# Moving VectorE work between slots in a fused spectral filter and two-layer GELU network, and one tile's second layer without the seven-product scheme

## The chip, the cores and the metric

The kernel runs on one core of a Trainium2 chip. The metric is device time in microseconds (us). The time before is 750.82 us, the median of three runs (750.49 to 752.01). A profiled execution of the same program took 750.39 us, and its span, from the first instruction to the last, is 748.6 us. Engines are named as in the profile: PE is TensorE's matmul, PEld its weight load, DVE is VectorE, ACT is ScalarE, POOL is GpSimd and SP is SyncE. "L468" is line 468 of the kernel before.

## The reference

```
x: 8 x 3008 x 256, filt_r and filt_i: 1505 x 256, w_in: 256 x 2048, w_out: 2048 x 256
X = rfft(x, axis=1);  Y = X * (filt_r + 1j*filt_i);  y = irfft(Y, n=3008, axis=1)
h = y.reshape(24064, 256) @ w_in
g = 0.5 * h * (1 + erf(h / sqrt(2)))
out = g @ w_out
```

## The kernel before

**Tiles and slots.** The Fourier transforms are matmuls with tables, in stages: 3008 = 47 x 64. The two layers run over 47 tiles of 512 tokens. A tile's first layer is 16 pieces (`mm1`, L637): two 128x512 matmuls into a PSUM bank of the pool "h" (three banks), and a gelu on ACT (L640) into `g_sb`. Each piece is a *slot*; slot 16*t + jc holds piece jc of tile t, and beside it a share of the second layer of tile t-1. In a slot first the steps that `put` listed for it are issued, then the second layer's share, then `mm1`. All engines take their instructions in the order of issue, and nothing reorders them.

**Second layer.** Tile 0 goes through `mm2_first` (L642): 64 matmuls of 256 columns, into two banks of the pool "o" (two banks), which L654 copies out. Every other tile goes through `mm2_seven`: the product is cut into two by two blocks and made with seven block products, 112 matmuls of 128 columns (L709), seven to a slot. For it VectorE forms sums of `g_sb` (`sums_1` L678 four times, `sums_2` L684 twice, `sums_3` L691 twice a tile) and adds the products up (L724, L726, L729, L731, L732, L735 and L738 twice a tile), which also frees the "o" banks. `put_rows` (L756) stores 128 rows at a time through the queue of SP or POOL.

**Spectral stages.** Batch 0 is transformed before slot 0. Batches 1 to 7 are spread over the slots, and are wanted by the tile that holds their rows; `first(b)` is the first slot of that tile. For a batch b:
- `load_next` (POOL) fetches x of the following batch; a tiny copy, `gate` (L146), makes POOL wait for a product of the unit before it starts a load.
- `fold` (L107 and L108, four per batch) forms sum and difference of two halves of x on VectorE.
- `s1` (L430, four per batch) is the first matmul stage; VectorE (L328) and ACT evict it, and SP stores it to DRAM. `r1` reads it back in another order (`b_sb`).
- `s2` (L457, three units per batch) is the second stage. It fills one "h" bank and all three banks of the pool "f". `s2_out` (four per unit) multiplies each bank with the filter (L468, into tiles `p`), and after the second of a pair forms the complex product sums (L471 and L472).
- `s3` (L485, one per unit) is the first inverse stage, again into one "h" bank and three "f" banks; `s3_out` evicts two banks at a time on ACT (L326; one bank of batch 1's unit 1 on VectorE) and stores them through SP. `r2` reads them back (`d_sb`).
- `s4` (L512, 16 per batch) is the last stage, into one "f" bank each; it is evicted by ACT or VectorE into `y_sb`, which `mm1` reads.

`s2[u]` below is the slot of unit u's s2. Before, s2 of batch 1 stands at slots 33, 45 and 57, and s3 at 42, 55 and 66. For batches 3 to 6 the units are 16 slots apart and s3 comes 10 slots after s2.

**Tables.** `table_4_all` builds the last stage's table on POOL (L411 and L413), in four parts of two pieces. A piece is two multiplications and an addition of 96x376, so a part is six POOL instructions. The four parts stand at slots 15, 80, 96 and 112. Their temporary tile comes from the pool that `d_sb` uses.

Of the kernel before, what the change touches and what calls it, by code (L numbers as in the profile page):

```python
# [22 lines left out]
TCH = 512  # L23
# [8 lines left out]
class _Mix:  # L32
# [428 lines left out]
    def s2_out(self, b, u, m, d):  # L461

        if d == 0:
            self.st[b, "p", 2 * u + m] = self.pp.tile([128, 2, 2, 2, 256], BF16, tag="p12", name="p12")
        w, a, v = self.st[b, "p", 2 * u + m], m ^ d, self.nc.vector.tensor_tensor
        ps = self.st[b, "ps2"][m][d].rearrange("p (r c) -> p r c", r=2)
        f = self.Fu[:, :, a, 2 * u + m, :]
        v(out=w[:, a], in0=ps.unsqueeze(2).to_broadcast([128, 2, 2, 256]),  # L468
          in1=f.unsqueeze(1).to_broadcast([128, 2, 2, 256]), op=ALU.mult)
        if d:  # L470
            v(out=w[:, :, 0, 0], in0=w[:, :, 0, 0], in1=w[:, :, 1, 1], op=ALU.subtract)  # L471
            v(out=w[:, :, 0, 1], in0=w[:, :, 0, 1], in1=w[:, :, 1, 0], op=ALU.add)  # L472

    def s3(self, b, u):

# [163 lines left out]
            o += n  # L639
        nc.scalar.activation(out=self.st["g", t][:, jc, :], in_=ps, func=AF.Gelu)  # L640

    def mm2_first(self, lo, hi):  # L642

        nc = self.nc
        for n in range(lo, hi):
            jc, q = (n // 2, n % 2) if n < 32 else (n % 16, n // 16)
            if n < 2:
                self.st["o2", q] = self.bank("ps_o", "o").rearrange("p (a b) -> p a b", a=2)
            ps = self.st["o2", q % 2]
            nc.tensor.matmul(ps[:, q // 2, :], lhsT=self.st["g", 0][:, jc, q * 128:q * 128 + 128],  # L650
                             rhs=self.w_out_sb[:, jc, :], start=(jc == 0), stop=(jc == 15))
# [41 lines left out]
    def mm2_seven(self, t, lo, hi):  # L693
# [9 lines left out]
        for n in range(lo, hi):  # L703
# [19 lines left out]
            if m == 0:  # L723
                nc.vector.tensor_copy(out=t1, in_=p1)  # L724
            elif m == 2:
                v(out=c(0, 0), in0=t1, in1=p0, op=ALU.add)  # L726
                if last:
                    self.store(t, 0, 0, nc.sync)
                v(out=t1, in0=t1, in1=p1, op=ALU.add)  # L729
            elif m == 4:  # L730
                v(out=t3, in0=t1, in1=p0, op=ALU.subtract)  # L731
                v(out=c(1, 1), in0=t3, in1=p1, op=ALU.add)  # L732
                if last:
                    self.store(t, 1, 1, nc.scalar)
                v(out=t1, in0=t1, in1=p1, op=ALU.add)  # L735
            else:
                for h, tt, p in ((1, t3, p0), (0, t1, p1)):
                    v(out=c(h, 1 - h), in0=tt, in1=p, op=ALU.add)  # L738
                    for sub in range(2):
                        self.put_rows(t * TCH + 256 * h + 128 * sub, self.st["c"][h][:, sub],  # L740
                                      nc.gpsimd if t > 1 or h > sub else nc.sync)
# [36 lines left out]
def kernel(  # L778
# [134 lines left out]
    for b in range(1, B):  # L913
        hi = first(b)
        e = 4 * (b == B - 1)
        s1, n1, r1 = (4, 2.75, 16) if b == 1 else (hi - 87, 3.7, hi - 73) if b == 2 else (hi - 94 - e, 3.7, hi - 80 - e)
        s2 = (33, 45, 57) if b == 1 else (hi - 64 - 2 * e + (b == 2), hi - 48 - 3 * e + e // 4, hi - 32 - 3 * e)
        busy.update(range(s1 - 1, s1 + int(3 * n1) + 2))
        for c in range(4):
            slot = s1 + int(c * n1 + (b == 1 and c in (1, 2)))  # L920
            put((0, 1, 5, 8)[c] if b == 1 else (67, 69, 86, 94)[c] if b == 2 else s1 - 28 + e + 6 * c, m.fold, b, c)
            put(slot, m.s1, b, c)
        for u in range(3):
            put(r1 if u < 2 else s2[0] + 1, m.r1, b, u)
            put(s2[u], m.s2, b, u)
            for i in range(4):
                put(s2[u] + ((0, 2, 5, 6)[i] if b == u == 1 else 2 * i + (b == 2 and u == 0)), m.s2_out, b, u, i // 2, i % 2)
            s3 = s2[u] + (9 if b == 1 and u != 1 else 10)
            put(s3, m.s3, b, u)
            put(s3 + 1, m.s3_out, b, u, 1)  # L930
            busy.update(range(s2[u] - 1, s2[u] + 5), range(s3 - 1, s3 + 2))
        after[b] = s3 + (5 if b > 1 else 4)
        crowd.update(range(s2[0], after[b]), range(s1 + 66, s1 + 94))
        if b + 1 < B:
            for i, (u, o, p) in enumerate(((0, 5, 1), (0, 7, 1), (1, 1, 2), (1, 5, 3), (1, 7, 3), (2, 1, 4), (2, 5, 5), (2, 7, 5))):
# [30 lines left out]
    put(14, m.table_4_factors, g)  # L966
    put(18, m.table_u)
    parts = [(w, h) for w in range(0, HB, 8) for h in range(2)]
    for i, slot in enumerate((15, 80, 96, 112)):
        put(slot, m.table_4_all, parts[2 * i:2 * i + 2])  # L970
    put(1, m.load_filters_again, nc.gpsimd, 0, 2)
    put(18, m.load_filters_again, nc.sync, 2, 4)
    put(20, m.weight_sums)
    seven = range(1, NT)
    for t in seven:
        for i, s in enumerate((12, 13, 15, 16 if t == S // TCH - 1 else 17)):
            put(16 * t + s, m.sums_1, t, 2 * i)
# [5 lines left out]
    for s in range((NT + 1) * 16):  # L983
# [43 lines left out]
```

## Time and profile before

| what | value |
|---|---|
| median of three runs | 750.82 us |
| profiled execution, its own time | 750.39 us |
| span of that execution | 748.6 us |
| PE busy | 730.8 us, 98% |
| PEld busy | 508.9 us, 68% |
| DVE busy | 616.9 us, 82% |
| ACT busy | 575.1 us, 77% |
| POOL busy | 288.2 us, 39% |
| granted TensorE clock | 1.00 |
| DMA | 89.31 MB, mean 119 GB/s |

A row of the costliest groups reads: line, engine, operation, what it writes and reads, the shape, how often, the busy time together, the mean duration of one, and the time the engine was idle just before such instructions with what ended most of it. A row of the timeline reads: start and length in us, engine, line, operation, tiles and shape, how many are merged into the row, and in brackets the idle time just before it and what ended it. Matmul durations overlap: the ends are modelled, and the next one starts long before the last one ends, so the rate is read from the starts.

### The profile page before, as it was taken

To read this page: it belongs to the slowest core of one execution; us is meant where nothing else is said; L and a number is where in the kernel's file an instruction comes from. 1 tells how busy PE (TensorE), PEld (TensorE's weight loads), DVE (VectorE), ACT (ScalarE), POOL (GpSimd) and SP (SyncE) were. 2 spreads that over 40 slices of the span, in tenths; PEclk is the share of its full clock that TensorE was granted. 3 is DMA by queue.
4 is the path that set the end of the run, shared out by engine and by line. 5 is a ranking of instruction groups with operands and counts; after the bars stand their busy time and mean duration, and the time that the engine had idled before them with its cause. 6 is when DMAs were issued, how large, how long until landed. Compare 5 with 4: busy or idle time off the path is not lost.

```text
span 748.6 us, 22400 instructions
## 1 busy us (share of the span) xinstructions
PE 730.8 (98%) x9261; PEld 508.9 (68%) x9261; DVE 616.9 (82%) x1120; ACT 575.1 (77%) x1048; POOL 288.2 (39%) x544
## 2 busy tenths in 40 slices
PE   8999999999999999999999999999999999999997
PEld 4856666666777667666677666666767766777776
DVE  8977998899887998789977989769997898676566
ACT  6987777677887788878887777877878787777773
POOL 7893446666122552234431355114631122112121
PEclk9999999999999999999999999999999999999999
DMA  9996542745345552546535455355444433301011
GB/s 154 213 193 185 125 109 86 212 90 123 86 121 177 117 119 82 142 148 134 112 103 162 111 126 131 90 158 129 117 108 118 153 91 99 117 31 58 29 57 58
DMA packets 81353, 89.31 MB, mean 119 GB/s; under 512 B 13171, under 2 KB 60659, under 8 KB 81251
## 3 DMA queue, kind: packets, MB, share of 16 engines
q0 software_dynamic: 22352, 39.76, 23.1%
q1 hardware_dynamic: 58483, 47.93, 22.8%
q8 instruction: 72, 1.18, 0.7%
q14 instruction: 30, 0.25, 0.1%
q10 hardware_dynamic: 416, 0.20, 0.1%
HBM read 55.57 MB, written 48.23 MB: 139 GB/s over the span
## 4 chain that ended last, share of the span: by engine, by line
PE 77%; DVE 15%; DMA 3%; POOL 2%; issue 2%; ACT 0%; DVEq 0%; POOLq 0%; SPq 0%
PE ps_h L637 35%; PE ps_o L709 33%; DVE p L468 5%; DMA x_sb<-in_x_dram 3%; PE ps_s L512 2%; PE ps_s L430 2%; DVE s_sb L678 2%; POOL out_dram L756 1%; PE ps_s L485 1%; DVE p L472 1%; PE ps_s L457 1%; DVE g_sb L684 1%; PE ps_o L650 1%; DVE s_sb L691 1%; DVE x_sb L108 1%
## 5 line engine op out<-in xcount | busy, mean ns | idle before, releaser
L640 ACT ACTIVATE g_sb<-ps_h 128x512 f16<-128x512 f32 x752 | 447.9, 603 | 146.1 <-PE ps_h L637 142.5
L637 PE MATMUL ps_h<-y_sb,w_in_sb 128*128 128x512 bf16 (+3 forms) x1600 | 445.3, 366 | 0.2 <-DVE a_sb L328 0.2
L756 POOL DMA_DIRECT2D out_dram<-ost x228 | 129.4, 574 | 389.3 <-DVE ost L738 359.4
L709 PEld LDWEIGHTS <-g_sb 128*128 128x128 f16 x2944 | 193.9, 98 | 90.1 <-issue 13.5
L709 PEld LDWEIGHTS <-s_sb 128*128 128x128 f16 x2208 | 147.8, 98 | 56.7 <-issue 3.7
L709 PE MATMUL ps_o<-w_sums,g_sb 128*128 128x128 f16 x1472 | 127.5, 219 | 4.7 <-DVE t_sb L729 3.5
L637 PEld LDWEIGHTS <-w_in_sb 128*128 128x128 bf16 x1600 | 125.0, 98 | 8.5 <-issue 1.1
L709 PE MATMUL ps_o<-w_sums,s_sb 128*128 128x128 f16 x1472 | 126.2, 219 | 0.1
L709 PE MATMUL ps_o<-w_out_sb,g_sb 128*128 128x128 f16 x1472 | 119.4, 219 | 2.1 <-DVE ost L738 2.1
L678 DVE TENSOR_TENSOR s_sb<-g_sb 128x1024 f16<-128x1024 f16 x184 | 120.3, 687 | 0.8 <-ACT g_sb L640 0.8
L468 DVE TENSOR_TENSOR p<-ps_s,F 128x1024 bf16<-128x1024 f32 x84 | 102.1, 1217 | 3.5 <-PE ps_s L457 1.8
L99 POOL DMA_DIRECT2D x_sb<-in_x_dram x156 | 79.0, 513 | 2.4 <-DMA x_sb<-in_x_dram 0.8
L684 DVE TENSOR_TENSOR g_sb<-s_sb,g_sb 128x1024 f16<-128x1024 f16 x92 | 65.0, 707 | 1.6
L709 PE MATMUL ps_o<-w_out_sb,s_sb 128*128 128x128 f16 x736 | 63.9, 219 | 0.0
L691 DVE TENSOR_TENSOR s_sb<-g_sb 128x1024 f16<-128x1024 f16 x92 | 63.8, 693 | 0.0
L731 DVE TENSOR_TENSOR t_sb<-t_sb,ps_o 128x256 f32<-128x256 f32 x46 | 19.3, 419 | 40.9 <-PE ps_o L709 39.7
L326 ACT ACTIVATE v_sb<-ps_s 128x512 bf16<-128x512 f32 x83 | 45.5, 608 | 6.3 <-PE ps_s L485 5.7
L326 ACT ACTIVATE y_sb<-ps_s 128x376 bf16<-128x376 f32 x94 | 46.6, 496 | 4.6 <-PE ps_s L512 4.6
L512 PEld LDWEIGHTS <-d_sb 96*128 96x128 bf16 x448 | 31.2, 97 | 27.2 <-issue 2.2
L738 DVE TENSOR_TENSOR ost<-t_sb,ps_o 128x256 f32<-128x256 f32 x90 | 33.7, 415 | 18.1 <-PE ps_o L709 18.1
L328 DVE CAST a_sb<-ps_s 128x512 bf16<-128x512 f32 x54 | 34.7, 684 | 12.7 <-PE ps_s L430 12.4
L726 DVE TENSOR_TENSOR ost<-t_sb,ps_o 128x256 f32<-128x256 f32 x46 | 19.1, 416 | 24.7 <-PE ps_o L709 24.1
(156 smaller groups left out, 556.7 us busy)
## 6 DMA issues: line engine op xcount, KB each, us to landing
out_dram<-ost POOLq DMA_DIRECT2D x126, 128.0 KB, 2.7
b_sb<-R SPq DMA_DIRECT2D x21, 512.0 KB, 5.2
R<-v_sb SPq DMA_DIRECT2D x84, 128.0 KB, 2.6
d_sb<-R SPq DMA_DIRECT2D x56, 192.0 KB, 3.3
R<-a_sb SPq DMA_DIRECT2D x108, 96.0 KB, 2.2
x_sb<-in_x_dram POOLq DMA_DIRECT2D x48, 94.0 KB, 2.7
x_sb<-in_x_dram POOLq DMA_DIRECT2D x48, 48.0 KB, 2.7
x_sb<-in_x_dram POOLq DMA_DIRECT2D x12, 188.0 KB, 5.1
```

What stands on the lines that cost most here:

```text
L99: self.nc.gpsimd.dma_start(out=xt[64 * v + to:64 * v + to + m, h, 4 * c:4 * c + 4 * n, :], in_=xv[h][at:at + m, w:w + 4 * n, :])
L326: self.nc.scalar.activation(out=out, in_=in_, func=AF.Copy, scale=1.0 if scale is None else scale)
L328: self.nc.vector.tensor_copy(out=out, in_=in_)
L468: v(out=w[:, a], in0=ps.unsqueeze(2).to_broadcast([128, 2, 2, 256]), in1=f.unsqueeze(1).to_broadcast([128, 2, 2, 256]), op=ALU.mult)
L512: nc.tensor.matmul(ps[:, 94 * i:94 * i + 94], lhsT=d[:, (grp % 2) * 4 + i, 128 * half:128 * half + 128], rhs=self.T4a[:, 4 * grp + i, 0:2 ...
L637: nc.tensor.matmul(ps[:, o:o + n], lhsT=w[:, dc], rhs=self.ring[:, dc, off:off + n], start=(dc == 0), stop=(dc == 1))
L640: nc.scalar.activation(out=self.st["g", t][:, jc, :], in_=ps, func=AF.Gelu)
L678: self.nc.vector.tensor_tensor(out=self.st["s", t][:, i:i + 2], in0=a, in1=b, op=ALU.subtract)
L684: self.nc.vector.tensor_tensor(out=a21[:, k], in0=self.st["s", t][:, k, 0], in1=a22[:, k], op=ALU.add)
L691: self.nc.vector.tensor_tensor(out=self.st["s4", t][:, k], in0=a12[:, k], in1=s2[:, k], op=ALU.subtract)
L709: nc.tensor.matmul(ps[:, (m + 1) % 2, sub, :], lhsT=a[:, i, 128 * sub:128 * sub + 128], rhs=b[:, i], start=i == 0, stop=i == 7)
L756: eng.dma_start(out=out, in_=tile_[lo - r0:lo - r0 + n])
```

## The change

Seven edits, in one diff:
- The product sums leave `s2_out` and become a step of their own, `s2_sum`. For batches 2 to 6 both pairs stand at s2 + 9 and s2 + 10, behind all four products; for batches 1 and 7 at s2 + 7 and s2 + 9.
- `s3` moves to s2 + 13 for batches 2 to 6 and to s2 + 11 for batches 1 and 7 (before: s2 + 10, or s2 + 9 for units 0 and 2 of batch 1). The last-stage steps around it move by a few slots, because the list of busy slots moves.
- Batch 1's units stand at slots 30, 43 and 56 in place of 33, 45 and 57, and lose an exception for unit 1's products.
- The folds move: for batch 2 the first two from slots 67 and 69 to 70 and 74; for later batches to 20, 13, 8 and 6 slots before `first(b)` - 94, where they were 28, 22, 16 and 10 before s1.
- The last three table parts move from slots 80, 96 and 112 to 22, 45 and 52.
- Tile 2's second layer goes through `mm2_first`, four matmuls of 256 columns a slot, and needs no sums; its rows are stored through POOL.
- Of tile 1's row blocks three go through POOL's queue and one through SP's (before: one and three).

```diff
@@ s2_out
-        if d:
-            v(out=w[:, :, 0, 0], in0=w[:, :, 0, 0], in1=w[:, :, 1, 1], op=ALU.subtract)
-            v(out=w[:, :, 0, 1], in0=w[:, :, 0, 1], in1=w[:, :, 1, 0], op=ALU.add)
+
+    def s2_sum(self, b, p):
+
+        w, v = self.st[b, "p", p], self.nc.vector.tensor_tensor
+        v(out=w[:, :, 0, 0], in0=w[:, :, 0, 0], in1=w[:, :, 1, 1], op=ALU.subtract)
+        v(out=w[:, :, 0, 1], in0=w[:, :, 0, 1], in1=w[:, :, 1, 0], op=ALU.add)
@@ mm2_first
-    def mm2_first(self, lo, hi):
+    def mm2_first(self, t, lo, hi):
...
-            jc, q = (n // 2, n % 2) if n < 32 else (n % 16, n // 16)
-            if n < 2:
-                self.st["o2", q] = self.bank("ps_o", "o").rearrange("p (a b) -> p a b", a=2)
-            ps = self.st["o2", q % 2]
-            nc.tensor.matmul(ps[:, q // 2, :], lhsT=self.st["g", 0][:, jc, q * 128:q * 128 + 128],
+            if t:
+                q, jc = n // 16, n % 16
+            else:
+                jc, q = (n // 2, n % 2) if n < 32 else (n % 16, n // 16)
+            if jc == 0 and (q % 2 == 0 if t else q < 2):
+                self.st["o2", q // 2 if t else q] = self.bank("ps_o", "o").rearrange("p (a b) -> p a b", a=2)
+            ps, a = (self.st["o2", q // 2], q % 2) if t else (self.st["o2", q % 2], q // 2)
+            nc.tensor.matmul(ps[:, a, :], lhsT=self.st["g", t][:, jc, q * 128:q * 128 + 128],
                              rhs=self.w_out_sb[:, jc, :], start=(jc == 0), stop=(jc == 15))
-            if q > 1 and jc == 15:
+            if jc == 15 and (q % 2 if t else q > 1):
                 ost = self.po.tile([128, 2, 256], FP32, tag="ost", name="ost")
                 nc.vector.tensor_copy(out=ost, in_=ps)
-                for a in range(2):
-                    self.put_rows((q - 2 + 2 * a) * 128, ost[:, a], nc.sync)
+                for i in range(2):
+                    self.put_rows(t * TCH + ((q - 1 + i) if t else (q - 2 + 2 * i)) * 128, ost[:, i],
+                                  nc.gpsimd if t else nc.sync)
@@ mm2_seven
-                                      nc.gpsimd if t > 1 or h > sub else nc.sync)
+                                      nc.gpsimd if t > 1 or h * sub == 0 else nc.sync)
@@ the slots of a batch
-        s2 = (33, 45, 57) if b == 1 else (hi - 64 - 2 * e + (b == 2), hi - 48 - 3 * e + e // 4, hi - 32 - 3 * e)
+        s2 = (30, 43, 56) if b == 1 else (hi - 64 - 2 * e + (b == 2), hi - 48 - 3 * e + e // 4, hi - 32 - 3 * e)
...
-            put((0, 1, 5, 8)[c] if b == 1 else (67, 69, 86, 94)[c] if b == 2 else s1 - 28 + e + 6 * c, m.fold, b, c)
+            put((0, 1, 5, 8)[c] if b == 1 else (70, 74, 86, 94)[c] if b == 2 else hi - 94 - (20, 13, 8, 6)[c], m.fold, b, c)
...
-                put(s2[u] + ((0, 2, 5, 6)[i] if b == u == 1 else 2 * i + (b == 2 and u == 0)), m.s2_out, b, u, i // 2, i % 2)
-            s3 = s2[u] + (9 if b == 1 and u != 1 else 10)
+                put(s2[u] + 2 * i + (b == 2 and u == 0), m.s2_out, b, u, i // 2, i % 2)
+            for i in range(2):
+                put(s2[u] + (9 + i if 1 < b < B - 1 else 7 + 2 * i), m.s2_sum, b, 2 * u + i)
+            s3 = s2[u] + (13 if 1 < b < B - 1 else 11)
...
-        after[b] = s3 + (5 if b > 1 else 4)
+        after[b] = s3 + 4
@@ tables and tiles
-    for i, slot in enumerate((15, 80, 96, 112)):
+    for i, slot in enumerate((15, 22, 45, 52)):
...
-    seven = range(1, NT)
+    plain = (0, 2)
+    seven = [t for t in range(NT) if t not in plain]
...
-            m.mm2_first(n(s), n(s + 1))
+            m.mm2_first(0, n(s), n(s + 1))
+        elif t - 1 in plain:
+            m.mm2_first(t - 1, 4 * jc, 4 * jc + 4)
```

In the kernel after the change, `after[b]` (the slot where `r2` starts reading back) is 71 for batch 1 and, for batches 2 to 6, 161, 257, 353, 449 and 545; it was 70, 159, 255, 351, 447 and 543.

## The prediction

> **What bounds the kernel now.** I read the page's first part, then the busy time by stretch, then TensorE's timeline wherever a stretch falls short, and last the timelines of the engine named there.
>
> ```profile
> PE 730.8 (98%) x9261; PEld 508.9 (68%) x9261; DVE 616.9 (82%) x1120; ACT 575.1 (77%) x1048; POOL 288.2 (39%) x544
> ...
> 60.00:100.00 40.00, 37.90 (x522) 24.15 (x520) 36.86 (x62) 27.67 (x50) 13.25 (x28) 1.00 0.54 127
> 145.00:190.00 45.00, 42.53 (x595) 28.99 (x588) 42.51 (x70) 33.54 (x63) 29.06 (x54) 1.00 0.56 129
> 190.00:237.00 47.00, 47.00 (x599) 34.20 (x597) 36.10 (x70) 37.81 (x69) 9.47 (x17) 1.00 0.41 121
> ```
>
> Columns of the stretches: length, then busy PE, PEld, DVE, ACT, POOL, granted clock, DMA share, GB/s. TensorE is the bound: from 190 to 237 us it never rests. It falls short where VectorE is nearly full (36.86 of 40, 42.51 of 45). So only stalls of TensorE can be won, and TensorE's order of work is fixed: a stall removed shortens the end by itself.
>
> ```profile
> 89.74 0.91 PE L457 MATMUL ps_s<-b_sb,T2p 64*32 64x256 bf16 x32
> 134.03 0.51 PE L709 MATMUL ps_o<-w_sums,g_sb 128*128 128x128 f16 x6 [0.71 <-DVE g_sb L684]
> 153.63 0.33 PE L512 MATMUL ps_s<-T4a,d_sb 96*128 96x94 bf16 x4 [1.69 <-DVE p L468]
> 260.62 0.93 PE L485 MATMUL ps_s<-p,U 32*64 32x256 bf16 x32
> 276.10 0.75 PE L485 MATMUL ps_s<-p,U 32*64 32x256 bf16 x32
> 278.65 0.38 PE L709 MATMUL ps_o<-w_sums,g_sb 128*128 128x128 f16 x4 [0.71 <-DVE t_sb L729]
> ```
>
> In TensorE's timeline a bracket is idle time. Seven 128-column matmuls start within 0.39 us (56 ns each), while one lasts 219 ns, so a bracket hides another 0.16 us of the previous matmul's tail: 0.71 costs 0.87. A group that runs long shows a wait inside it: s3 takes 0.75 unhindered and 0.93 when it waits for the product sums.
>
> ```profile
> 131.42 2.55 DVE L684 TENSOR_TENSOR g_sb<-s_sb,g_sb 128x1024 f16<-128x1024 f16 x1
> 366.32 0.42 DVE L472 TENSOR_TENSOR p<-p 128x512 bf16<-128x512 bf16 x1
> 366.65 0.68 DVE L107 TENSOR_TENSOR xs<-x_sb 111x1024 bf16<-111x1024 bf16 x1
> 367.37 0.69 DVE L108 TENSOR_TENSOR x_sb<-x_sb 111x1024 bf16<-111x1024 bf16 x1
> 367.98 0.41 DVE L726 TENSOR_TENSOR ost<-t_sb,ps_o 128x256 f32<-128x256 f32 x1
> 368.43 0.42 DVE L729 TENSOR_TENSOR t_sb<-t_sb,ps_o 128x256 f32<-128x256 f32 x1
> ...
> 131.79 1.61 POOL L411 TENSOR_TENSOR tmp_sb<-t_sb 96x376 f32<-96x376 f32 x2
> 75.84 1.11 ACT L326 ACTIVATE v_sb<-ps_s 128x512 bf16<-128x512 f32 x2
> ```
>
> These name the causes. A sum of 0.69 took 2.55 beside POOL's table part, and TensorE lost 0.87 at 133 us. In each steady batch, sums and a fold stand ahead of the L726/L729 additions that free a PSUM bank.
>
> Stalls in the TensorE timeline, in us: **A** (60 to 100 us, batch 1) 0.79+0.42, 0.75, 0.71, 0.28, 0.34, 0.90 = 4.2. **B** (100 to 145) 0.59, 0.33, 0.87 = 1.8. **C** (145 to 190, batch 2) 1.85, 0.28, 0.17, 0.18, 0.17, 0.18, 0.87 = 3.7. **D** (batches 3 to 6) per batch one 0.87, one or two s3 waits of 0.18, as many waits of 0.17 for L724: 1.2+1.6+1.6+1.6 = 5.9, the batch-3 one smaller. **E** (batch 7) 0.06+0.89 = 0.95. Together 16.6.
>
> **The change, part by part.** VectorE issue distances, from starts in its timeline: L468 product 1.14, L471+L472 0.70, L678/L684/L691 0.60, a fold's two 1.33, the 256-column L7xx ones 0.34, the 512-column copy 0.60. TensorE's slot (two 512-column and seven 128-column matmuls) 0.82.
>
> *Tile 2 direct.* Removes 112 matmuls x 0.056 = 6.24 and adds 64 of 256 columns, which start 0.109 apart in tile 0 (L650): 6.98. Cost **+0.75** on TensorE. On VectorE 8 sums and 10 evacuations leave, two copies come: 4.8+3.4-1.2 = 7.0 us less between slots 44 and 64, where its work (by these prices about 42 us over slots 28 to 72, as much as TensorE's 42) was the bound. [...]
>
> *Batch 1's units at 30, 43, 56; s3 at +11.* s2 at slot 30 falls at 62.2; its b_sb landed by 60.98, so it doesn't wait. VectorE then has from 62.65: four products 4.6, tile 0's copy 0.6, four sums 2.4, L724 0.34, the first product sums 0.70, L691 0.6, L726/L729 0.75, second sums 0.70 = 10.7, to 73.35. POOL's second table part, now at slot 22, runs at 60 to 66 beside them. Parts delayed VectorE by 0.83 (L678 pair 2.11 instead of 1.28), 0.9 and 2.0 in before; I take 0.85, bounds 0 and 2.0. So the sums end at 74.2, s3's half follows to 74.7, wanted at 71.5+0.95: stall 2.2 (1.4 to 3.4). Next, s2 stands two slots after s3. It needs s3's last banks, which ACT empties as two evictions, a gelu, two evictions, 0.48 each. In before unit 2 was two slots behind s3 and L457 took 0.91 instead of 0.63, with the last eviction on VectorE; with it on ACT as here 0.28+0.48 = 0.76 (bounds 0.28 and 0.96, one gelu more). Unit 2 keeps VectorE's help: 0.2. Its second sums come 6.7 after slot 60, s3 wants them at 6.4: 0.35, plus 0.85 for the part moved to slot 52, which POOL reaches at about 90 behind part 45, a gate, loads and tile 1's rows: 1.2 (0.35 to 2.3). A after: 2.2+0.76+0.2+1.2+0.75 = 5.1 against 4.2: **+0.9** (-1.2 to +3.4).
>
> *Table parts gone from slots 80, 96, 112.* The 0.33 and 0.87 of B go; 0.59 is gelu to L678 to L684 to TensorE and stays: **-1.2** (-0.5 to -1.3).
>
> *Product sums behind all four products, s3 at +13 (batches 2 to 6).* The four sums (1.4) now stand behind L468, L726, L729, L691; from s2 on VectorE has 4.6 of products, three sums before the tile and two L691 3.0, L724 0.34, L726/L729 0.75, and then these 1.4 = 10.1, and TensorE takes 11.7 to s3 (s2 0.65, 13 slots 10.7, two s4 0.34), so L724's 0.17, s3's 0.18 and L729's 0.87 go. L729 would be late again only if four sums and a fold still stood ahead. What is late next is the next s2, three slots behind s3 (it was six). Such a spacing exists in before: s3 ended at 74.31, s2 started at 76.88, the last ACT eviction ended at 76.95, and s2 took its usual 0.63. I take 0.05 each for eight, D: 5.9-0.4 = **-5.5** (-5.9; or -1.6 if each costs one ACT eviction more, 0.48). Batch 2's first pair has only two slots: 0.76, and s4 at slots 118 to 124 follows the products that free its banks: 0.2 (0 to 0.9). C **-2.7** (-3.5 to -1.8).
>
> *Batch 7, sums at +7 and +9, s3 at +11.* One sum pair less ahead of L738 (0.89 to 0.2); a two-slot pair costs 0.76: E **0.0** (-0.8 to +0.5).
>
> *Folds* stay 14 slots or more ahead of s1, where VectorE's work over eight slots (five sums, a fold, L738 twice, L724) is 6.0 of TensorE's 6.6: 0. If that cover went, 1.33 would land on L738. *Queues:* tile 1's three row stores leave SP for POOL and wait behind part 45 (6.2 us); their four-deep ost buffers are wanted again at about 99, after landing by 91. POOL's gates and x loads behind them move some 8 us; the chunks wanted by the fold at slot 74 were loaded with gate 48, by 93: 0. SP loses a wait for L738. r2 is two slots later, and d_sb landed at 375.5 for s4 at 382.2, so 3 us remain: 0.
>
> [...]
>
> Sum: 0.9-1.2-2.7-5.5+0.0 = -8.5. From the profiled execution's 750.39 (span 748.6 and 1.8 around it) this is **741.9**; the median of the runs, 750.82, is 0.4 above that execution.
>
> **Rivals.** (1) *The steady gain half fails:* the L729 wait stays (4 x 0.87) and A ends at its worse bound (+2.5 more): 741.9+6.0 = 747.9. For it: four sums and two folds are only moved. Against: the order puts the sums after L726/L729. (2) *No gain:* the three-slot spacing costs 0.9 at each of nine places, 750. (3) *Slower:* s3's banks bind. The mechanism is one: ACT empties them too late for s2. If s4's evictions two slots earlier leave ACT two instructions and a gelu behind (1.44 at nine places, 13.0, less the 0.4 counted), the time is 754.5. It decides from 1.0 us per place (8.5/9 and the 0.05). Against: ACT rests 0.23 before nearly every gelu, and 76.88 shows no wait. (4) *More gain:* POOL meets no two-input sum, A at -1.2 and C, D, E at their lower ends: -12.7, 737.7.
>
> **How the numbers follow.** Forecast with its own range 738 to 745.5: 0.68. Rival 1 0.12, rival 2 0.05, rival 3 0.10, rival 4 0.05. Runs here differ by 0.2% (1.5 us), about what can be told from no change. Faster takes the forecast, rivals 1 and 4 less some of rival 1: 0.82; same 0.06; slower 0.12. Range 738 to 748: it leaves rivals 2 and 3 and a tail below.
>
> **What would show it.** s3 groups of 0.75 in batches 3 to 6 with no bracket on L729; no L684 of 2.5 at 130; L457 near 1.4 in the two-slot places and 0.63 to 0.7 in the three-slot ones; a bracket of 1 to 2 us at batch 1's first s3. Wrong if L457 runs long everywhere, if s4's L512 waits for d_sb, or if A loses more than 3.

## The result and the profile after

The changed kernel takes 741.12 us (median of four runs, 740.40 to 741.93). The kernel before has 751.41 us over four runs (the three given above and one of 752.26). The ratio is 0.9864 with a 95% interval of 0.9846 to 0.9881, so the change saves 10.3 us or 1.4% (9.7 us against the 750.82 of the first three). The profiled execution of the changed kernel took 740.78 us, its span is 739.0 us.

The line numbers move a little in the changed kernel: mm1 is L640, its gelu L643, the seven-product matmul L716, `s3` L488, `s4` L515, the product sums L474 and L475, `sums_1` to `sums_3` L685, L691 and L698, the additions of the seven-product scheme L731 to L745 (L736 was L729, L745 was L738), and `r2` L506. `s2` stays L457 and the product with the filter stays L468.

First the busy times of the changed kernel, from the page's first part:

```profile
PE 716.6 (97%) x9063; PEld 506.7 (69%) x9213; DVE 604.0 (82%) x1105; ACT 575.6 (78%) x1049; POOL 290.8 (39%) x547
```

Then its busy time by stretch, for the stretches that the prediction read and two more (columns as there: length, PE, PEld, DVE, ACT, POOL, granted clock, DMA share, GB/s):

```profile
60.00:100.00 40.00, 37.10 (x447) 24.03 (x462) 33.62 (x47) 27.00 (x48) 31.86 (x48) 1.00 0.47 116
100.00:145.00 45.00, 42.92 (x532) 29.23 (x535) 35.30 (x68) 34.26 (x64) 13.84 (x28) 1.00 0.52 141
145.00:190.00 45.00, 44.11 (x615) 30.97 (x625) 41.55 (x73) 36.27 (x68) 22.93 (x47) 1.00 0.56 120
190.00:237.00 47.00, 46.63 (x591) 34.21 (x596) 37.01 (x69) 37.03 (x69) 11.81 (x21) 1.00 0.47 137
```

From 145 to 190 us TensorE now works 44.11 of 45 us where it had 42.53, while VectorE is as full as it was (41.55 against 42.51): VectorE's work there is hardly less, it stands in another order. From 60 to 145 us VectorE has clearly less to do (33.62 and 35.30, before 36.86 and 38.01), POOL in the first of these stretches 18.6 us more, and TensorE does not gain. (TensorE's sums are a little low in these rows, since 150 matmul records, 146 of them of L640, are missing from this trace.)

Starts of the gelus give a sharper view, because slot N is the same piece of work in both kernels. The table is worked out from the gelu rows of the two timelines:

| part of the span | before | after | difference | forecast |
|---|---|---|---|---|
| start to slot 0 | 38.34 | 38.57 | +0.24 | 0 |
| slots 0 to 16 | 14.55 | 14.12 | -0.43 | 0 |
| A, slots 16 to 67 | 49.62 | 49.00 | -0.62 | +0.9 |
| B, slots 67 to 112 | 42.11 | 42.50 | +0.39 | -1.2 |
| C, slots 112 to 168 | 55.25 | 52.29 | -2.96 | -2.7 |
| D, slots 168 to 576 | 385.03 | 378.93 | -6.10 | -5.5 |
| E, slots 576 to 640 | 59.78 | 60.40 | +0.62 | 0.0 |
| slots 640 to 751 | 93.69 | 93.69 | 0.00 | 0 |
| last gelu to the end | 10.22 | 9.49 | -0.73 | 0 |
| span | 748.59 | 739.00 | -9.59 | -8.5 |

The last row but one is no gain of the mechanism: the last matmuls and stores are issued at the same distance from the last gelu in both kernels, and only the time from the last store's issue to the end of the span differs. That tail is 9.97 to 10.63 us in the three profiles built on the kernel before, 9.47 to 9.49 in ten of the eleven built on the changed kernel and 10.06 in the other; whether this is chance stays open. The first two rows scatter (38.3 to 39.9 and 14.1 to 15.2 us over the 14 profiles of this study). Without the three, 8.67 us are gained where 8.5 were forecast.

One border of the table is unfair. Gelu 67 starts 1.31 us after the first weight load of its own `mm1` in the kernel before and 0.75 us in the changed one, because ACT is later there. Taken at the weight load, so on TensorE's side, A is 0.06 us shorter and B 0.17 us shorter; their sum is the same.

What is left of TensorE's waits in the changed kernel, from its timeline (start, length, tiles, number of matmuls merged, and in brackets the idle time and its end):

```profile
69.17 0.51 PE L716 MATMUL ps_o<-w_sums,g_sb 128*128 128x128 f16 x6 [0.99 <-DVE g_sb L691]
74.15 0.65 PE L488 MATMUL ps_s<-p,U 32*64 32x256 bf16 x16 [0.88 <-DVE p L474]
77.42 0.41 PE L457 MATMUL ps_s<-b_sb,T2p 64*32 64x256 bf16 x15 [0.22 <-ACT v_sb L326]
89.61 0.82 PE L457 MATMUL ps_s<-b_sb,T2p 64*32 64x256 bf16 x32
114.68 0.33 PE L515 MATMUL ps_s<-T4a,d_sb 96*128 96x94 bf16 x4 [1.65 <-DMA d_sb<-R]
158.57 0.72 PE L457 MATMUL ps_s<-b_sb,T2p 64*32 64x256 bf16 x17
159.51 0.41 PE L457 MATMUL ps_s<-b_sb,T2p 64*32 64x256 bf16 x15 [0.22 <-ACT v_sb L326]
259.45 0.64 PE L488 MATMUL ps_s<-p,U 32*64 32x256 bf16 x32
262.59 0.63 PE L457 MATMUL ps_s<-b_sb,T2p 64*32 64x256 bf16 x32
551.73 0.33 PE L515 MATMUL ps_s<-T4a,d_sb 96*128 96x94 bf16 x4 [0.51 <-DMA d_sb<-R]
591.32 0.45 PE L716 MATMUL ps_o<-w_out_sb,g_sb 128*128 128x128 f16 x5 [0.66 <-DVE ost L745]
```

In the steady batches the waits of before are gone: `s3` takes 0.64 us at 259.45, and `s2`, three slots behind it, 0.63 us at 262.59. One small wait per batch is new: the `s4` at 267.48 starts 0.2 us late, just after the product L468 that ends at 267.43. The two-slot pairs at 77 and 159 wait for ACT; the one at 159 takes 1.35 us from 158.57 to 159.92 (two rows), 0.72 more than the 0.63 of an unhindered group. Two waits are of a kind that the profile of before did not have: `s4` waits for the DMA that brings `d_sb`, at 114.68 and 551.73.

VectorE's timeline of the changed kernel in batch 3 shows the order that does it:

```profile
256.14 0.42 DVE L736 TENSOR_TENSOR t_sb<-t_sb,ps_o 128x256 f32<-128x256 f32 x1
256.47 0.69 DVE L698 TENSOR_TENSOR s_sb<-g_sb 128x1024 f16<-128x1024 f16 x1
257.08 0.42 DVE L474 TENSOR_TENSOR p<-p 128x512 bf16<-128x512 bf16 x1
...
258.08 0.42 DVE L475 TENSOR_TENSOR p<-p 128x512 bf16<-128x512 bf16 x1
```

L736, the second of the two additions that free the PSUM bank, comes first; the four product sums (two rows left out) follow and end at 258.5, 0.95 us before `s3` wants them at 259.45.

### The profile page after: what moved, and what is told of

Read it like the earlier page. It is cut to its first block, busy times and chain, and to the rows that moved or that the text cites. A ratio compares the mean times of both kernels' runs of the same rounds, so it can differ in the third digit from the quotient of the medians.

```text
span 739.0 us, 22144 instructions
## 1 busy us (share of the span) xinstructions
PE 716.6 (97%) x9063; PEld 506.7 (69%) x9213; DVE 604.0 (82%) x1105; ACT 575.6 (78%) x1049; POOL 290.8 (39%) x547
## 4 chain that ended last, share of the span: by engine, by line
PE 87%; ACT 4%; DVE 3%; DMA 3%; issue 2%; POOL 0%; SPq 0%; another core or an unknown queue 0%; DVEq 0%; POOLq 0%; ACTq 0%
PE ps_o L716 38%; PE ps_h L640 37%; PE ps_s L515 3%; PE ps_s L430 2%; PE ps_o L656 2%; ACT g_sb L643 2%; PE ps_s L457 2%; PE ps_s L488 2%; DMA R<-v_sb 1%; ACT v_sb L326 1%; DVE p L468 1%; DMA d_sb<-R 1%; DMA x_sb<-in_x_dram 1%; PE ps_c L587 1%; ACT y_sb L326 1%
## 5 line engine op out<-in xcount | busy, mean ns | idle before, releaser
L643 ACT ACTIVATE g_sb<-ps_h 128x512 f16<-128x512 f32 x752 | 445.8, 603 | 141.1 <-PE ps_h L640 116.5
L640 PE MATMUL ps_h<-y_sb,w_in_sb 128*128 128x512 bf16 (+3 forms) x1454 | 414.4, 365 | 0.6
L763 POOL DMA_DIRECT2D out_dram<-ost x231 | 131.2, 575 | 398.5 <-DVE ost L745 390.0
L716 PEld LDWEIGHTS <-g_sb 128*128 128x128 f16 x2880 | 189.0, 98 | 84.5 <-issue 13.5
L716 PEld LDWEIGHTS <-s_sb 128*128 128x128 f16 x2160 | 145.0, 98 | 53.6 <-issue 3.7
L640 PEld LDWEIGHTS <-w_in_sb 128*128 128x128 bf16 x1600 | 125.7, 98 | 7.7 <-issue 1.3
L716 PE MATMUL ps_o<-w_sums,g_sb 128*128 128x128 f16 x1440 | 124.8, 220 | 2.4 <-DVE g_sb L691 1.0
L716 PE MATMUL ps_o<-w_sums,s_sb 128*128 128x128 f16 x1440 | 123.4, 219 | 1.7 <-DVE t_sb L731 0.2
L685 DVE TENSOR_TENSOR s_sb<-g_sb 128x1024 f16<-128x1024 f16 x180 | 119.5, 696 | 0.7 <-ACT g_sb L643 0.6
L716 PE MATMUL ps_o<-w_out_sb,g_sb 128*128 128x128 f16 x1440 | 116.5, 220 | 2.5 <-DVE ost L745 0.7
L468 DVE TENSOR_TENSOR p<-ps_s,F 128x1024 bf16<-128x1024 f32 x84 | 102.0, 1218 | 7.8 <-PE ps_s L457 6.2
L716 PE MATMUL ps_o<-w_out_sb,s_sb 128*128 128x128 f16 x720 | 62.5, 219 | 0.9
L691 DVE TENSOR_TENSOR g_sb<-s_sb,g_sb 128x1024 f16<-128x1024 f16 x90 | 62.1, 691 | 1.5
L698 DVE TENSOR_TENSOR s_sb<-g_sb 128x1024 f16<-128x1024 f16 x90 | 61.5, 683 | 0.0
L738 DVE TENSOR_TENSOR t_sb<-t_sb,ps_o 128x256 f32<-128x256 f32 x45 | 18.8, 419 | 41.6 <-PE ps_o L716 41.1
L515 PEld LDWEIGHTS <-d_sb 96*128 96x128 bf16 x448 | 31.2, 97 | 28.6 <-DMA d_sb<-R 2.8
L745 DVE TENSOR_TENSOR ost<-t_sb,ps_o 128x256 f32<-128x256 f32 x88 | 32.9, 416 | 15.6 <-PE ps_o L716 15.6
```

The costliest lines, as they stand in the source:

```text
L515: nc.tensor.matmul(ps[:, 94 * i:94 * i + 94], lhsT=d[:, (grp % 2) * 4 + i, 128 * half:128 * half + 128], rhs=self.T4a[:, 4 * grp + i, 0:2 ...
L640: nc.tensor.matmul(ps[:, o:o + n], lhsT=w[:, dc], rhs=self.ring[:, dc, off:off + n], start=(dc == 0), stop=(dc == 1))
L685: self.nc.vector.tensor_tensor(out=self.st["s", t][:, i:i + 2], in0=a, in1=b, op=ALU.subtract)
L691: self.nc.vector.tensor_tensor(out=a21[:, k], in0=self.st["s", t][:, k, 0], in1=a22[:, k], op=ALU.add)
L698: self.nc.vector.tensor_tensor(out=self.st["s4", t][:, k], in0=a12[:, k], in1=s2[:, k], op=ALU.subtract)
L716: nc.tensor.matmul(ps[:, (m + 1) % 2, sub, :], lhsT=a[:, i, 128 * sub:128 * sub + 128], rhs=b[:, i], start=i == 0, stop=i == 7)
```

## The experiments

All kernels but the first two start from the changed kernel. A median is given with that of the kernel before from the same session. The latter moved between 750.88 and 751.41 us from session to session, so a difference of medians from two sessions is good to about 0.5 us. Parts of the span are those of the table above.

**The product sums alone** (`sums_only`): the kernel before, with nothing changed but the sums of batches 2 to 6.

```diff
+            mid = 1 < b < B - 1
+            for i in range(2 if mid else 0):
+                put(s2[u] + 9 + i, m.s2_sum, b, 2 * u + i)
+            s3 = s2[u] + (13 if mid else 9 if b == 1 and u != 1 else 10)
...
-        after[b] = s3 + (5 if b > 1 else 4)
+        after[b] = s3 + (5 if b == B - 1 else 4)
```

> The kernel before, with the product sums of batches 2 to 6 behind all four products and s3 at s2 + 13; folds, tables, batch 1, batch 7 and tile 2 as before. Theory (the sums ahead of L726/L729 and right before s3 make the waits): the D waits go as in the forecast (-5.5 us), and of batch 2 the three s3 waits, two L724 waits and the L729 wait (1.75 together) less one two-slot s2 (0.6): about -6.6, 744.5 to 745. Rival (the fold ahead of L726/L729 makes the largest wait, and it stays where it was here): the five waits of 0.87 for L729 stay, so about -2.3, 749.

Measured: 743.24 us (before 751.05; ratio 0.9893, 0.9878 to 0.9908), 7.8 us of the 10.3, and 1.3 below the theory's range; the rival is out. Part D is 379.66 us, 5.37 less than before, and C 52.92, 2.33 less; A and B stay within 0.25 us of before. In its TensorE timeline the waits for L729 are gone, with the folds still at their old slots:

```profile
171.04 0.64 PE L490 MATMUL ps_s<-p,U 32*64 32x256 bf16 x32
...
191.24 0.45 PE L714 MATMUL ps_o<-w_out_sb,g_sb 128*128 128x128 f16 x5 [0.28 <-DVE ost L743]
```

A bracket of 0.28 (0.44 us with the hidden tail) remains at the end of a tile, at 191 and twice later, where a fold delays L743 (L738 in before). So the step of the sums carries most of the change, and the folds are not needed to free L729. The sums and the three slots by which `s3` moves come together here; no run has `s3` later alone.

**The table parts alone** (`tables_only`): the kernel before, with one line changed.

```diff
-    for i, slot in enumerate((15, 80, 96, 112)):
+    for i, slot in enumerate((15, 22, 45, 52)):
```

> The kernel before with one line changed: the three late table parts at slots 22, 45 and 52, where the prediction put -1.2 us on stretch B. Theory (the parts collide wherever VectorE is full): the waits of L729 at 113 and 121 and part of the one at 99 go (-1.2 to -1.8 us), but the parts of slots 22 and 45 stretch VectorE's work between 62 and 90 us, where the seven-product group of tile 2 still stands in this kernel, and TensorE waits 1 to 3 us more there. Sum -0.5 to +2: 750.5 to 753. Rival (the tables cost nothing in their new slots, as the prediction had it but for one 1.2 us wait): no new wait before slot 64, 749.3 to 749.9.

Measured: 752.99 us (before 750.88; ratio 1.0029, 1.0019 to 1.0039), slower by 2.1 us, at the upper end of the theory's range and far from the rival. A takes 55.35 us, 5.7 more than before, where the theory had 1 to 3; B 0.35 less and C 1.7 less. TensorE, VectorE and POOL in this kernel's timelines:

```profile
76.06 1.11 PE L485 MATMUL ps_s<-p,U 32*64 32x256 bf16 x26 [1.44 <-DVE p L468]
87.29 0.45 PE L709 MATMUL ps_o<-w_out_sb,g_sb 128*128 128x128 f16 x5 [2.00 <-DVE ost L738]
104.08 1.11 PE L485 MATMUL ps_s<-p,U 32*64 32x256 bf16 x26 [0.82 <-DVE p L468]
106.14 0.71 PE L709 MATMUL ps_o<-w_out_sb,g_sb 128*128 128x128 f16 x5 [0.74 <-DVE ost L738]
```

```profile
76.72 2.75 DVE L691 TENSOR_TENSOR s_sb<-g_sb 128x1024 f16<-128x1024 f16 x1
```

```profile
77.29 1.61 POOL L411 TENSOR_TENSOR tmp_sb<-t_sb 96x376 f32<-96x376 f32 x2
78.98 1.33 POOL L413 TENSOR_TENSOR T4a<-tmp_sb 96x376 bf16<-96x376 f32 x1
```

The sum, elsewhere 0.68 us, starts at 76.72 and lasts until 79.47, past both L411 and into L413. VectorE falls behind over this stretch, and L738 holds TensorE for 2.00 us at 87. The new slots are no place with little VectorE work in this kernel; in the changed kernel, with tile 2's second layer off VectorE, they still cost A 1.2 us (`tables_back` below).

**Tile 2 back to seven products** (`tile2_seven`):

```diff
-    plain = (0, 2)
+    plain = (0,)
```

> The kernel after, with tile 2's second layer through the seven products again. Theory (VectorE is the bound of batch 1's stretch): TensorE saves 0.75, but VectorE has 7.0 us more between slots 44 and 64 and TensorE waits for it again, 2 to 4 us, so +1.3 to +3.3, 742.4 to 744.4. Rival (VectorE has room there since the sums and tables moved): only the 0.75 is left, 740.4.

Measured: 743.21 us (before 751.05; ratio 0.9894, 0.9879 to 0.9908), 2.1 us more than the changed kernel and inside the theory's range. A is 3.6 us longer; B is 1.2 shorter, as this profile lacks the wait for `d_sb`. VectorE is late at three places of A, of which the changed kernel has the first (0.99 us there):

```profile
70.47 0.51 PE L716 MATMUL ps_o<-w_sums,g_sb 128*128 128x128 f16 x6 [1.28 <-DVE g_sb L691]
86.29 0.45 PE L716 MATMUL ps_o<-w_out_sb,g_sb 128*128 128x128 f16 x5 [1.17 <-DVE ost L745]
103.37 0.45 PE L716 MATMUL ps_o<-w_out_sb,g_sb 128*128 128x128 f16 x5 [1.00 <-DVE ost L745]
```

The direct layer costs TensorE 0.75 us by its rates and is worth 2.1 net.

**The folds back** (`folds_back`):

```diff
-            put(... (70, 74, 86, 94)[c] if b == 2 else hi - 94 - (20, 13, 8, 6)[c], m.fold, b, c)
+            put(... (67, 69, 86, 94)[c] if b == 2 else s1 - 28 + e + 6 * c, m.fold, b, c)
```

> The kernel after, with the folds at their old slots. Theory (sums): without the sums ahead of it a fold alone doesn't make L729 late, so at most +0.5, 741 to 741.6. Rival (folds): the L729 wait of 0.87 comes back in five batches, +4.4, 745.5.

Measured: 742.67 us (before 751.05; ratio 0.9886, 0.9871 to 0.9901), 1.5 us more, above the theory and far from the rival. L736 is not late. What comes back is one wait at the end of a tile in batches 2, 5 and 6, as in `sums_only`:

```profile
190.71 0.45 PE L716 MATMUL ps_o<-w_out_sb,g_sb 128*128 128x128 f16 x5 [0.27 <-DVE ost L745]
```

Three of 0.44 are 1.3 us. C and D are 0.62 and 1.19 us longer than in the changed kernel. The old and the new slots of the folds both leave L729 alone; the new ones also clear the tile's end.

**The table parts back** (`tables_back`):

```diff
-    for i, slot in enumerate((15, 22, 45, 52)):
+    for i, slot in enumerate((15, 80, 96, 112)):
```

> The kernel after with the table parts back at slots 15, 80, 96 and 112, all else as in after. Prediction's step: the moved parts were worth 1.2 us, so 742.3. Theory now (a part costs where it is put, as long as VectorE has little slack there): the 1.15 us wait at 68 and the 1.82 us wait for the second-spectrum transfer at 113 go, the 0.59 us wait under the latter shows again, and one or two waits of 0.3 to 0.9 us come back between 113 and 135 us. Sum -2.4 +0.6 to 1.5: 739.3 to 740.2.

Measured: 741.74 us (before 750.98; ratio 0.9873, 0.9859 to 0.9887), between the prediction's 742.3 and the theory's 739.3 to 740.2. Its interval overlaps that of the changed kernel: the ratios differ by 0.0009, and their half-widths, 0.0014 and 0.0018, give 0.0023 as the root of their squares' sum, so the move of the tables within the whole change is worth 0.7 us, give or take 1.7. That stays open. By the profile the expected exchange took place: A is 1.2 us shorter (the wait at 68 is gone), and at 133 us TensorE waits again 0.86 for an L691 that took 2.71 us beside POOL's L411. The 1.2 us of the forecast's step B are not there as a net gain.

**The last table part at slot 102** (`part4_late`):

```diff
-    for i, slot in enumerate((15, 22, 45, 52)):
+    for i, slot in enumerate((15, 22, 45, 102)):
```

> The kernel after, with the last table part at slot 102 in place of 52. Theory (the part holds POOL, so ten loads of x and three row stores are issued in one bunch while s3's stores to DRAM of batch 1's last unit are on their way; these land 7 us after issue, and the first s4 waits 1.8 us for d_sb): without the bunch they land within 5 us, the s4 wait falls to 0 to 0.6, and the 0.6 wait for L691 that it had covered may show; -1.2 to -1.8, 739.3 to 739.9. Rival (the wait comes of s3 standing one slot later and of TensorE running ahead, not of the bunch): the wait stays, 741.1.

Measured: 741.10 us (before 751.05; ratio 0.9862, 0.9846 to 0.9879), no change. That is the rival's number, but not its mechanism: the wait for `d_sb` at 114 went, and others came. POOL's loads were no longer behind the part. SyncE's rows of the changed kernel, of this one:

```profile
101.84 2.57 SPq L498 DMA_DIRECT2D R<-v_sb  x4
111.09 0.84 SPq L506 DMA_DIRECT2D d_sb<-R  x2
```

```profile
102.19 2.55 SPq L498 DMA_DIRECT2D R<-v_sb  x4
106.58 0.94 SPq L506 DMA_DIRECT2D d_sb<-R  x2
```

The stores start at the same time, but the read that waits for them starts at 111.09 in the changed kernel and at 106.58 here. The DMA share of the changed kernel in between is 0.97 (0.74 here):

```profile
103.00:106.00 3.00, 3.00 (x37) 2.21 (x35) 2.90 (x7) 2.61 (x6) 3.00 (x7) 1.00 0.97 184
```

because POOL, held by the table part from 90.88 to 97.2, then issues its queue at once:

```profile
90.88 1.62 POOL L411 TENSOR_TENSOR tmp_sb<-t_sb 96x376 f32<-96x376 f32 x2
...
96.23 0.98 POOL L413 TENSOR_TENSOR T4a<-tmp_sb 96x376 bf16<-96x376 f32 x1
97.16 1.84 POOL L763 DMA_DIRECT2D out_dram<-ost  x3
99.61 2.08 POOL L99 DMA_DIRECT2D x_sb<-in_x_dram  x4
...
103.14 1.98 POOL L99 DMA_DIRECT2D x_sb<-in_x_dram  x4
```

This bunch makes the read late, but not alone a wait of TensorE. The profiles of `folds_back`, `s3_earlier` and `tile2_seven` have the same table slots and such a bunch; there the read starts 6.9, 6.3 and 5.7 us after the first store, against 9.3 in the changed kernel and 4.4 without the bunch (here and in `tables_gated`), and `s4` does not wait. The last 2 us in the changed kernel, from 109.00 to 111.09, pass with a DMA share of 0.08; why the last store landed so late stays open.

And the part at slot 102 landed on VectorE again, 0.62 us of idle TensorE at 133.77 behind an L691 of 2.51 us.

**Two parts behind a gate** (`tables_gated`): the last two parts wait for a copy that VectorE makes in the seven-product group, so that POOL can't run them ahead.

```diff
+    def table_4_gated(self, parts):
+        self.gate(self.st["t"][0:1, 0, 0, 0:1])
+        self.table_4_all(parts)
...
-    for i, slot in enumerate((15, 22, 45, 52)):
-        put(slot, m.table_4_all, parts[2 * i:2 * i + 2])
+    for i, slot in enumerate((15, 45, 67, 99)):
+        put(slot, m.table_4_gated if i > 1 else m.table_4_all, parts[2 * i:2 * i + 2])
```

> The kernel after with the table parts at slots 15, 45, 67 and 99, the last two each behind a copy of one element that waits for a transition copy of tile 1 or 2, so that GpSimd can't run them ahead. Theory: the wait of 1.15 us at 68 goes, and the wait of L515 for its second-spectrum transfer at 113 (1.82 us) goes with it, since GpSimd's loads are no longer issued in a bunch; the 0.59 us wait that this one hid shows again. Sum -1.5 to -2.3 us: 738.8 to 739.6. Rival (the parts carry their cost along, as the part put at slot 102 did): new waits of 0.8 to 1.2 us where they now stand, 740.5 to 741.5.

Measured: 739.59 us (before 750.88; ratio 0.9847, 0.983 to 0.9863), 1.5 us less than the changed kernel, the smallest gain that the theory allowed; the intervals still overlap. Both waits are gone (A -1.2 us, B -0.64). In place of the second TensorE is idle 0.49 us at 112.71 for L750 (L745 in the changed kernel) and 0.20 us at 114.52 for the sums, which the wait for `d_sb` had covered.

**Three slots where there were two** (`s3_earlier`):

```diff
-                put(s2[u] + (9 + i if 1 < b < B - 1 else 7 + 2 * i), m.s2_sum, b, 2 * u + i)
-            s3 = s2[u] + (13 if 1 < b < B - 1 else 11)
+                put(s2[u] + (9 + i if 1 < b < B - 1 else 7 + i if b > 1 and u == 0 else 7 + 2 * i), m.s2_sum, b, 2 * u + i)
+            s3 = s2[u] + (13 if 1 < b < B - 1 else 11) - (u == 0 and b in (2, B - 1))
```

> The kernel after with the first unit's third stage one slot earlier in batches 2 and 7, so that three slots and not two lie between it and the next unit's second stage. Theory: the two waits of 0.58 us at 159 and 595 go, as no three-slot group waits in the kernel after: -1.2 us, 740.0. Rival (the product sums are not done one slot earlier): the third stage waits for VectorE instead, 0.3 to 0.6 us each, 741.1 and no gain.

Measured: 740.13 us (before 750.88; ratio 0.9854, 0.9839 to 0.9868). The medians differ by 1.0 us and the intervals overlap; the profile decides. Both `s2` groups take 0.63 now, but in batch 7 the third stage waits in their place:

```profile
157.94 0.63 PE L457 MATMUL ps_s<-b_sb,T2p 64*32 64x256 bf16 x32
...
590.59 0.65 PE L488 MATMUL ps_s<-p,U 32*64 32x256 bf16 x16 [0.75 <-DVE p L474]
593.74 0.63 PE L457 MATMUL ps_s<-b_sb,T2p 64*32 64x256 bf16 x32
```

C is 1.05 us shorter, as in `combined` and the two kernels after it: 0.72 is the pair, which the theory had at 0.58, and 0.2 is a fourth-stage step that now falls in B. E, with its pair's 0.72 gone and the wait for L745 too, is only 0.2 shorter. The theory held in batch 2 and the rival in batch 7.

**Both of these** (`combined`):

The edits are the last two diffs together.

> Both of the last two edits in one kernel. If both theories hold, their gains add: -2.7 to -3.5 us, 737.6 to 738.4. If both rivals hold, 740.5 to 741.5. If only the spacing holds, 739.3 to 740.3.

Measured: 739.11 us (before 750.88; ratio 0.9842, 0.9828 to 0.9857), 2.0 us less than the changed kernel: less than the sum of the theories (2.7); the two measured gains (1.5 and 1.0) add up to more, but within the noise of the medians. Batch 7 is one reason; another is the wait for batch 6's `d_sb`, 1.24 us in this profile where the changed kernel has 0.67.

**Batch 1's units three slots later** (`units_back`):

```diff
-        s2 = (30, 43, 56) if b == 1 else ...
+        s2 = (33, 46, 59) if b == 1 else ...
```

> The kernel after with batch 1's units three slots later (33, 46 and 59), their spacing kept. Theory: the third unit's row stores and the second-spectrum transfer come three slots (2.8 us) later while the fourth stage keeps its slot, so that the wait of L515 near 113 grows from 1.8 to some 4 us, less up to 1.2 us where the third stage of the first unit no longer waits for its sums near 73: 742.5 to 744. Rival (the earlier slots are worth nothing, since the slack of that chain takes them): 740.5 to 741.5.

Measured: 742.40 us (before 750.98; ratio 0.9882, 0.9867 to 0.9897), 1.3 us more and just under the theory's range, but not for its reason: the wait for `d_sb` fell to 0.22 us. The loss is at 77 us, where the table part of slot 45 meets the first unit's sums. TensorE, VectorE and the clock:

```profile
77.92 0.32 PE L488 MATMUL ps_s<-p,U 32*64 32x256 bf16 x8 [1.74 <-DVE p L474]
78.88 0.32 PE L488 MATMUL ps_s<-p,U 32*64 32x256 bf16 x8 [0.65 <-DVE p L475]
```

```profile
76.83 1.04 DVE L474 TENSOR_TENSOR p<-p 128x512 bf16<-128x512 bf16 x1
77.79 1.04 DVE L475 TENSOR_TENSOR p<-p 128x512 bf16<-128x512 bf16 x1
```

```profile
77.00:79.00 2.00, 0.43 (x16) 0.24 (x15) 2.00 (x3) 0.00 (x0) 1.92 (x3) 1.00 0.24 34
79.00:80.00 1.00, 1.00 (x16) 0.88 (x11) 0.91 (x3) 0.79 (x2) 0.92 (x2) 0.58 0.00 0
...
82.00:83.00 1.00, 1.00 (x34) 0.36 (x32) 0.04 (x1) 0.97 (x3) 0.41 (x1) 0.72 0.65 150
```

Two sums of 0.41 took 1.04 each, and the granted clock (the last column but two) fell after the waits. The theory named the wrong late chain.

**A version that beats both** (`combined2`): `combined` with two edits more.

```diff
-        s2 = (30, 43, 56) if b == 1 else ...
+        s2 = (30, 44, 57) if b == 1 else ...
...
-            s3 = s2[u] + (13 if 1 < b < B - 1 else 11) - (u == 0 and b in (2, B - 1))
+            s3 = s2[u] + (13 if 1 < b < B - 1 else 11) - ((u == 0 and b in (2, B - 1)) or (u == 2 and b == B - 2))
```

> The kernel with gated tables and the two earlier third stages, and two more edits: batch 1's second and third units one slot later (30, 44, 57), and the third stage of batch 6's last unit one slot earlier. Theory: the 0.58 us wait at 76.9 goes (three slots there too), and the wait of 1.1 to 1.2 us for batch 6's second-spectrum transfer near 549 falls to 0.2 to 0.4, since the transfer starts a slot of 0.92 us earlier: 739.1 - 1.4 = 737.7. Rival (the transfer is late because it shares the DMA engines with five row stores, which follow it wherever it goes; the later units delay batch 1's chain): 738.7 to 739.5.

Measured: 737.63 us (median of five runs, 736.81 to 738.17; before 750.98; ratio 0.9819, 0.9805 to 0.9834), against 737.7 by the theory. This is the fastest kernel of the study, 3.5 us below the changed one, and their intervals are apart. Two rows of its timeline answer the two edits:

```profile
76.08 0.63 PE L462 MATMUL ps_s<-b_sb,T2p 64*32 64x256 bf16 x32
```

```profile
542.75 1.31 SPq L511 DMA_DIRECT2D d_sb<-R  x2
```

Three slots behind `s3`, batch 1's second `s2` takes 0.63. And batch 6's `d_sb` is fetched at 542.75 (548.33 in the changed kernel, whose slots are 3.2 us later by then); `s4` no longer waits for it, and D is 378.25 us against 379.49 in `combined`. Moving this chain by one slot took the whole wait and not a slot's worth, as its last store then has a start on the five stores of a tile's rows: it is issued 1.1 us ahead of the first of them and lands in 2.4 us, where in `combined` it is issued 0.1 us ahead and lands in 4.3. The wait is missing in `combined3` too, which has this edit; without it one profile of nine built on the changed kernel's order (`tile2_seven`) lacks it as well, so a part of this may be chance.

**One slot further** (`combined3`): as `combined2`, with batch 1's units at 30, 45 and 58 and its first `s3` at slot 42.

```diff
-        s2 = (30, 44, 57) if b == 1 else ...
+        s2 = (30, 45, 58) if b == 1 else ...
...
-            ... - ((u == 0 and b in (2, B - 1)) or (u == 2 and b == B - 2))
+            ... - ((u == 0 and b in (2, B - 1)) or (u == 2 and b == B - 2)) + (b == 1 and u == 0)
```

> As the last, but batch 1's units at 30, 45 and 58 with the first unit's third stage at slot 42 in place of 41. Theory: the third stage's wait of 1.03 us for its product sums near 73 falls to 0.1 to 0.2 on top: 736.9. Rival (the chain of batch 1, two slots later, makes the fourth stage wait at 113): 737.7 to 739.

Measured: 739.60 us (before 750.98; ratio 0.9847, 0.9832 to 0.9862), 2.0 us worse than `combined2` and above what either theory gave. The first unit's `s3` still waits 0.34 and 0.83 us, and the third unit's takes 3.11 us in place of 0.64, with idle times of 0.27 and 1.78, as its last product sum meets the gated table part. VectorE and POOL:

```profile
101.55 2.17 DVE L480 TENSOR_TENSOR p<-p 128x512 bf16<-128x512 bf16 x1
```

```profile
101.84 1.60 POOL L411 TENSOR_TENSOR tmp_sb<-t_sb 96x376 f32<-96x376 f32 x2
```

## Why the prediction was right, and where its steps were off

The forecast was 741.9 us; 741.12 were measured, inside its range. The main mechanism holds: TensorE's order is fixed, the waits of batches 2 to 6 came from sums standing ahead of L726 and L729, and the sums behind them cost nothing. That the total came within 1 us is partly luck: by TensorE's borders A came out 1.0 below its forecast and B 1.0 above, and D 0.6 below and E 0.6 above.

- **Batches 3 to 6 (D), -5.5 forecast, -6.1 measured.** `sums_only` has -5.4 with the sums alone. Their working held, with the sizes off. `s3` takes 0.64, so the 0.75 that the prediction called unhindered still held 0.11 of waiting, twelve times, and the waits of before come to some 7.5 us, not 5.9 (in `s3` eight of 0.28 and four of 0.11, eight of 0.17 for L724, four of 0.87). The three-slot `s2` took 0.63 everywhere, not 0.05 more. What is left is a wait of 0.2 per batch for the product ahead of one `s4`, and 0.67 for `d_sb` in batch 6. For the latter the prediction saw 3 us in hand, in another batch; even there, `d_sb` lands at 374.79 for the `s4` at 375.49, so 0.7 remain.
- **Folds, 0 forecast.** With the folds at their old slots the kernel is 1.5 us slower, about 1.3 of it a wait for L745. The prediction named that addition (L738) as the one to suffer, but took the old slots as no worse; that was wrong.
- **Batch 2 (C), -2.7 forecast, -3.0 measured.** The two-slot pair costs 0.72, and 0.76 was taken. Its cause is what was named: ACT empties `s3`'s last banks late. `s3_earlier` shows it, for with three slots it is gone. The waits of before, with 0.64 for `s3`, were 3.9 and not 3.7.
- **Batch 1 (A), +0.9 forecast, -0.6 measured (-0.1 by TensorE's border).** The chain to the first `s3` went as described but its waits were 1.15 and 0.35 us at 68 to 71 and 1.31 in `s3` itself (1.95 in place of 0.64), 2.8 in all against 2.2; the two-slot `s2` costs 0.72 and the third unit's 0.19, as forecast (0.76 and 0.2). The failed term is the third unit's `s3`, 1.2: it takes 0.79 in place of 0.64, a wait of 0.15. The part did stretch the sums there (0.97 for a 0.42 at 96.5), but VectorE still ended the last at 100.3, while `s3` ran from 99.88 on. And the waits of before, taken with 0.64 for `s3`, were 4.6 and not 4.2. The direct second layer of tile 2 is inside A; turned back, A loses 3.6.
- **Table parts (B), -1.2 forecast, +0.4 measured (-0.2 by TensorE's border).** This is the step that failed. The waits at 121 and 133 went as foreseen, and also the one at 113, but 1.82 us of waiting for `d_sb` came instead. The prediction asked whether the gates and loads moved on POOL's queue delay the folds that want them, and put the queues at 0; it did not ask what the bunched transfers delay. Without the bunch the read of `d_sb` starts 4.4 us after the first store (`part4_late`, `tables_gated`), with it 5.7 to 9.3; that the longest of these has a second cause is not excluded. Only one of the four profiles with these table and unit slots has the wait: `folds_back`, `s3_earlier` and `tile2_seven` lack it, and B takes 41.30 to 41.52 us there. So by the table this step was worth between +0.4 and -0.8 in these profiles.
- **Batch 7 (E), 0.0 forecast, +0.6 measured.** The two-slot pair costs 0.72, near the 0.76 taken, but L745 is as late as before (0.82): the one sum pair less ahead of it did not bring the 0.7 that the forecast took.
- **A part's price on VectorE, 0.85 taken, bounds 0 and 2.0.** In the changed kernel it is 1.05 (0.97 and 1.46 us for two sums of 0.69), 1.27 and 1.17. These three lie inside the bounds; one sum alone lost up to 2.07 (2.75 for 0.68), in `tables_only`.

Of the rivals, the first (L729 stays) falls with `sums_only`. The second and third (the three-slot spacing costs 0.9 or more, ACT empties the banks too late) fall with rows of 0.63 in all steady batches; the third's mechanism is real at two slots, at 0.72. The fourth (more gain) took place in part: A came out below its forecast, though POOL does meet two-input sums (0.97 us for a 0.42 at 96.5).

Beside a table part the changed kernel shows the product L468, with one input in PSUM, at 1.22 us from 64.90 on, while POOL's L411 runs from 64.41 to 66.45; that is the mean of its 84 (1.218). The two sums right behind it, beside the same part, took 0.97 and 1.46 in place of 0.69. The waits of such sums are longer than one POOL instruction here: in `tables_only` the sum of 2.75 us, from 76.72 to 79.47, spans two L411 (77.29 to 78.90, 1.61 together) and a part of an L413, so it did not get in between them.

## What to carry to other kernels

When TensorE's order is fixed and VectorE is nearly full, look first at what stands ahead of the instruction that frees a PSUM bank: four short sums moved behind it, with the stage that needs them three slots later, gave most of this gain (7.8 of 10.3 us in `sums_only`) without any work less. A step that moves on a queue in order takes what is queued behind it along, its transfers too (the part that held POOL from 90.88 to 97.2 us was followed at once, from 97.16 on, by the stores and loads listed behind it), so price where those land and not only the step itself. And a slot on a queue that runs ahead is only a place in the order (in `part4_late` POOL started the part of slot 102 at 131.53, 3.4 us before that slot's `mm1` at 134.94): what ought to run late needs something to wait for, as the copy in `tables_gated` that waited 0.75 us for VectorE before the part of slot 67.

## What the runs showed that was not expected

- **After some waits the clock fell, and they cost more than their idle time.** In `units_back` TensorE was busy 0.43 of the 2 us from 77 to 79, and the granted clock then fell to 0.50: a mean of 0.58 from 79 to 80 and of 0.72 from 82 to 83 puts the half clock between 79.2 and 82.6. `tables_only` shows the same after its waits of 0.82 and 0.74 us at 104 and 106, with means of 0.78 (105 to 107), 0.50 and 0.86 (109 to 111), so from 106.1 to 109.6. Over 3.4 us at half clock TensorE loses an estimated 1.7. A single wait of 2.00 us in `tables_only` and waits of 0.27 and 1.78 in `combined3` left the clock at 1.00, so the length of a wait doesn't decide. Nor does TensorE's busy time in the 3.4 us before, taken alone: it was 1.03 us in `units_back` (75.74 to 79.16) and 1.79 in `tables_only` (102.72 to 106.13), and 3.4 us of `tables_only` with 1.72 (85.65 to 89.07) left the clock at 1.00. What does was not measured.
- **A VectorE sum lasted over a whole run of POOL instructions**: 2.75 us in `tables_only` and 2.71 in `tables_back` for 0.68, and 2.17 in `combined3` for 0.42, each until after two L411 (1.60 to 1.61 us together) had ended.
- **Parts of the timing repeat to hundredths**: slots 640 to 751 take 93.69 us in all 14 profiles, while the first 16 slots take 14.07 to 15.20 in programs that are alike there. Two executions should be compared over stretches, and not only by their ends.
